# Two blocks' PV sums in one PSUM bank with one divide, and a later load of W2, in a two-layer sliding-window transformer kernel

## The chip, the cores and the metric

The kernel runs on one core of one Trainium2 chip. A core has TensorE (PE in profiles: matrix products out of SBUF into PSUM), VectorE (DVE), ScalarE (ACT), GpSimd (POOL) and SyncE (SP, which here issues all DMAs). The engines run side by side, each through its own instructions in order, and wait for each other on semaphores. The metric is the device time of one execution in microseconds (us), as the median of several runs.

## The reference

The same pair of layers is applied twice to x of 2048 rows by 512 columns: attention in a sliding window of 256 keys with 32 heads of 16, and a two-matrix block with a ReLU in between. Both follow a layer normalisation and are added to x.

```python
def _A_ref(x, wqkv, wo):                       # H = 32, Dh = 16, W = 256
    qkv = (x @ wqkv) -> q, k, v per head
    scores = einsum("bhqd,bhkd->bhqk", q, k) * (Dh ** -0.5)
    mask = (i - j >= 0) & (i - j < W)
    p = softmax(where(mask, scores, -1e9))
    return (p @ v, heads side by side) @ wo

def _B_ref(x, w1, w2):                         # Dff = 1792
    return relu(x @ w1) @ w2

x = x + _A_ref(layernorm(x), wqkv, wo)
x = x + _B_ref(layernorm(x), w1, w2)
x = x + _A_ref(layernorm(x), wqkv, wo)
x = x + _B_ref(layernorm(x), w1, w2)
```

Inputs and output are bfloat16; x is kept in float32 on the chip.

## The kernel before

**Tiles and stages.** The 2048 rows are cut into four chunks of 512. A step k = 0 to 7 is one chunk of one layer (k = 4 layer + chunk). Each step has three parts: `plan_qkv` (normalise, transpose, project to Q, K and V), `plan_attention`, and `plan_rest` (output projection wo, residual, normalise, transpose, W1 with ReLU, W2, residual). x, all weights, K and V stay in SBUF.

**Attention.** Heads are taken eight at a time (t = 0 to 3). A `Unit` is one t with all eight 64-row query blocks of a chunk, or, in the first and the last step, with four of them. Its scores come in up to five groups ("score blocks"), each of up to four times 512 columns in four PSUM banks (`Sps`). ScalarE takes the exponential of each block into one of two buffers `Pb`, which alternate from unit to unit. Triangular masks are laid over the edges by VectorE (a minimum with `tri`) or GpSimd (`affine_select`, two instructions for each edge). `pv_group` then multiplies with V: for each 128-row query block (`jl`, four in a full unit) and each of four head pairs p, up to six matmuls of 34 columns add into a tile `acc`. Columns 16 of each 17 hold the sums of the exponentials, since V carries a column of ones. `divide` (lines 393 to 398) takes the reciprocal of these sums into `chk` and multiplies 128 columns into `O`. Units are counted below from 0, in order of time.

**Transposes.** The normalised blocks `xn` (a pool of three buffers) are transposed by DMA into `xnT` and `xn2T`, the attention's output `O` into `OT`. Each is one `dma_start_transpose` on SP's queue, in the order in which SP stands. The first step's xn and the last step's O and xn go through TensorE instead (tiles `tp`).

**PSUM.** Four banks are for scores, four (pool `psum`, line 226) for everything else. A piece of work that needs one takes it at its first matmul and gives it back when the engine that empties it has finished. This holds for the accumulations over four or fourteen matmuls (`ps_d`), for the transposes and for `acc`.

**The order of the work.** A planner in the kernel makes it when the program is built. Each piece is an `Op` with a key, the engines that can do it with a cost in us, and what it depends on. The planner runs through time with these costs (lines 759 to 796): whenever an engine is free, it takes the ready piece with the lowest key. Score blocks and their exponentials have the lowest keys (-1e5), then PV sums (-5e4), final transposes, wo, then the projections and the W1 and W2 products, which fill what is left. Work that two engines can do (masks, copies out of PSUM, V copies, normalisations) goes to whichever comes first. When TensorE has had nothing for 0.4 us by the plan and more than one bank is free, a warming matmul on the identity (`warm`, 128 by 512) is put in until something is ready. On the chip, each engine then goes through its pieces in that order, whatever the real times. All instructions are made by one helper, so that profiles show them under line 106: tiles tell them apart.

**Loads.** SP issues them at the start in this order: x of chunk 0, the three parts of wqkv, x of the other chunks, wo, W1, W2 (lines 131 to 142). For the planner they land at fixed times (lines 237 to 240).

```python
d_wo, d_w1, d_w2 = landed(18.0), landed(24.0), landed(30.0)
...
box.ps = box.tile([P, 4, 2, 17], FP32, "acc")
```

In step 0, `plan_qkv(1)` comes right after the attention (line 676), so the normalised blocks of chunk 1 are the first that go through DMA transposes.

Of the kernel before, what the change touches and what calls it, by code (L numbers as in the profile page):

```python
# [9 lines left out]
FP32 = mybir.dt.float32  # L10
# [4 lines left out]
ALU = mybir.AluOpType  # L15
P = 128
# [46 lines left out]
def kernel(  # L63
# [51 lines left out]
    pe, dve, act, pool, sp = (InOrder(x) for x in (nc.tensor, nc.vector, nc.scalar, nc.gpsimd, nc.sync))  # L115

    def mm(o, lhsT, rhs, start, stop):
        pe.matmul(o, lhsT=lhsT, rhs=rhs, start=start, stop=stop)
# [20 lines left out]
    w1 = const.tile([P, KC, DFF], BF16, name="w1")  # L139
    sp.dma_start(w1[:], B_w1.rearrange("(kc p) n -> p kc n", p=P))  # L140
    w2 = const.tile([P, NF, D], BF16, name="w2")
    sp.dma_start(w2[:], B_w2.rearrange("(f p) n -> p f n", p=P))


    ident = const.tile([P, P], BF16, name="ident")
# [41 lines left out]
    SOON = {"qkv": 0, "v": 0, "h": 0, "mask": 0, "div": -1, "add": -1}  # L187
# [34 lines left out]
    def op(key, opts, deps=(), take=None, uses=(), keep=0):  # L222
        uses = list(uses) + ([take] if take is not None and take not in uses else [])
        return Op(key, opts, deps, take, uses, keep)
# [6 lines left out]
    def landed(t):  # L231
        o = Op(0, {}, [], None, [], 0)
        fixed.append((o, t))
        return o
# [2 lines left out]
    d_x = [landed(3.95), landed(4.5)]  # L237
    d_w = {1: landed(7.4), 0: landed(9.0), 2: landed(10.6)}
    d_xc = {c: landed(11.4 + 1.7 * c) for c in range(1, NCH)}
    d_wo, d_w1, d_w2 = landed(18.0), landed(24.0), landed(30.0)  # L240


    def copy(e, o, i, relu=False):
# [11 lines left out]
    def options(times, fn):  # L255
        return {e: (t, lambda e=e: fn(e)) for e, t in times.items()}
# [64 lines left out]
    def slot(layer, kb):  # L321
        return (32 * layer + kb) % NSLOT
# [20 lines left out]
    def score_group(u, g, Qt, pb, Sps):  # L343
        layer = u.k // NCH
        for kb, lo, n, at in u.groups[g]:
            sl = slot(layer, 8 * u.c + u.q0 + kb)
            for r in range(4):
                rows = slice(32 * r, 32 * r + 32)
                mm(Sps[:, r, 64 * at:64 * (at + n)], KBD[rows, u.t, sl].rearrange("p e k -> p (e k)"),
                   Qt[rows, 64 * (u.q0 + lo):64 * (u.q0 + lo + n)], True, True)  # L350

    def bounds(u, g):
        return 64 * min(b[3] for b in u.groups[g]), 64 * max(b[3] + b[2] for b in u.groups[g])

    def places(pb, g):
        return Pb[pb][:, 0:PWALL].rearrange("p (g r c) -> p g r c", g=5, r=4)[:, g]

    def exp_group(u, g, pb, Sps):
        a, z = bounds(u, g)
        act.activation(places(pb, g)[:, :, 64 + a:64 + z], Sps[:, :, a:z], ACT.Exp, scale=0.25)  # L360
# [21 lines left out]
    def seen(u, jl):  # L382
        return [kb for kb in range(2 * jl - 4, 2 * jl + 2) if u.c > 0 or kb + u.q0 >= 0]

    def pv_group(u, jl, p, pb, acc):
        kbs = seen(u, jl)
        for i, kb in enumerate(kbs):
            g, lo, at = u.place[kb]
            col = (4 * g + p) * PW + 64 + 64 * (at + 2 * jl - lo)
            mm(acc[:, p], Pb[pb][:, col:col + P], V2[:, slot(u.k // NCH, 8 * u.c + u.q0 + kb), :, 4 * u.t + p, :],  # L390
               i == 0, i == len(kbs) - 1)

    def divide(t, j, acc, O, chk):
        rinv = chk[:, j, 8 * t:8 * t + 8].rearrange("p (a e) -> p a e", e=2)
        dve.reciprocal(rinv, acc[:, :, :, 16])
        dve.tensor_tensor(out=O[:, j, P * t:P * (t + 1)].rearrange("p (a e d) -> p a e d", a=4, e=2),
                          in0=acc[:, :, :, 0:16],
                          in1=rinv.rearrange("p a (e o) -> p a e o", o=1).to_broadcast([P, 4, 2, 16]), op=ALU.mult)

    def accumulate_check(chk, first):  # L400
        mx = small.tile([P, 1], FP32, name="chk_mx")
# [27 lines left out]
    first_slot = {}  # L429
# [22 lines left out]
    scores, exps, masks, pvs, divs, checks = {}, {}, {}, {}, {}, []  # L452
    k_done, q_done, v_done, qkv_mm, w1_mm, w2_mm, x_done = {}, {}, {}, {}, {}, {}, {}
    applied, turned = {}, {}
    Q, xnTs, xn2T, hTs, O_of = {}, {}, {}, {}, {}

    def first(table, key, make):
        if key not in table:
            table[key] = make()
        return table[key]  # L460
# [71 lines left out]
    def plan_attention(k):  # L532
        layer, c = divmod(k, NCH)
        prev = units_of.get(k - 1, []) if c else []
        for n in units_of[k]:
            u = units[n]
            pb = n % 2
            before = [pvs[n - 2, j] for j in range(units[n - 2].nq // 2)] if n > 1 else [c_p[0], c_p[1]]
            for g in range(len(u.groups)):
                s = first_slot[n] + g  # L540
                h = u.q0 // 4 if k == 0 else 0
                need = [k_done[k, u.t, 0], q_done[k, u.t, h]] + ([k_done[k, u.t, 1]] if k == 0 and h else [])
                if c:
                    need += [k_done[k - 1, u.t, i] for i in range(2) if (k - 1, u.t, i) in k_done]
                cols = sum(b[2] for b in u.groups[g]) * 64
                a, z = bounds(u, g)
                cell = {}

                def sfn(u=u, g=g, pb=pb, cell=cell):
                    cell["S"] = ps_s.tile([P, 4, 512], FP32, name="Sps")  # L550
                    score_group(u, g, Q[u.k, u.t], pb, cell["S"])
                scores[s] = op(-1e5 + s, {"PE": (0.2 + 0.02 * len(u.groups[g]) + cols * 0.00042, sfn, 0.27 + 0.02 * len(u.groups[g]) + cols * 0.00042)},
                               need + ([exps[s - 1]] if s else []))
                exps[s] = op(-1e5, {"ACT": (0.168 + 0.00083 * 4 * (z - a), lambda u=u, g=g, pb=pb, cell=cell: exp_group(u, g, pb, cell["S"]))},
                             [scores[s]] + before)
                masks[s] = []
                for m in u.masks(g):
                    times = {"DVE": 0.32 + 0.14 * (len(m) - 1), "POOL": 0.93 * len(m)}
                    masks[s].append(op(SOON["mask"], options(times, lambda e, m=m, g=g, pb=pb: mask(e, m, places(pb, g))), [exps[s]] + c_tri))
            for jl in range(u.nq // 2):  # L560
                kbs = seen(u, jl)
                need = []
                for g in sorted({u.place[kb][0] for kb in kbs}):
                    need += [exps[first_slot[n] + g]] + masks[first_slot[n] + g]
                for kb in kbs:
                    b = u.q0 + kb
                    need.append(v_done[k, b // 2] if b >= 0 else v_done[k - 1, (b + 8) // 2])
                j = u.q0 // 2 + jl
                box = Box(psum)

                prior = None
                for p in range(4):
                    def pfn(u=u, jl=jl, pb=pb, box=box, p=p):
                        if p == 0:
                            box.ps = box.tile([P, 4, 2, 17], FP32, "acc")
                        pv_group(u, jl, p, pb, box.ps)
                    prior = op(-5e4 + n - (1000 if p else 0), {"PE": (0.025 * len(kbs) + (0.03 if p == 0 else 0.0), pfn)},
                               [prior] if p else need, None if p else box, [box])
                pvs[n, jl] = prior

                def dfn(u=u, j=j, box=box):
                    o = first(O_of, u.k, lambda: work.tile([P, 4, D], BF16, name="O", tag="O", bufs=1))
                    divide(u.t, j, box.ps, o, chks[u.k % 2])
                war = [turned[k - 1, i] for i in range(4)] if k else []
                divs[k, u.t, j] = op(SOON["div"], {"DVE": (0.5, dfn)}, [pvs[n, jl]] + war + checks[k - 2:k - 1], None, [box])
        checks.append(op(40, {"DVE": (1.1, lambda k=k: accumulate_check(chks[k % 2], k == 0))},
                         [divs[k, t, j] for t in range(4) for j in range(4)] + checks[-1:]))

# [84 lines left out]
    for k in range(NSTEP):  # L673
        plan_attention(k)
        if k == 0:
            plan_qkv(1)
        plan_rest(k)
        if 0 < k < NSTEP - 1:
            plan_qkv(k + 1)
# [80 lines left out]
    while events and events[0][0] < 3000:  # L760
        t, _, o, e = heapq.heappop(events)
# [15 lines left out]
        for e in ENGINES:  # L777
            if busy[e] > t + 1e-9:
                continue
            o = choose(e, t)  # L780
# [4 lines left out]
            elif e == "PE" and done_ops[0] < len(ops) - 12:  # L785
                if t - idle_since[0] >= (0.4 if t > 20 else 0.0) and sum(1 for f, _ in psum.free if f <= t) > 1:
                    box = Box(psum)
                    box.users = 1
                    d = Op(0, {"PE": (0.43 if t < 9 else 0.216, lambda: None)}, [], box, [], 0)
# [83 lines left out]
    with tc.If(flag > 0):  # L873
# [13 lines left out]
        for layer in range(2):  # L887
            for c in range(NCH):
# [13 lines left out]
                O = work.tile([P, 4, D], BF16, name="O", tag="O", bufs=1)  # L902
# [51 lines left out]
```

## Time and profile before

| what | us |
|---|---|
| median of 4 runs | 486.83 (486.37 to 487.46) |
| the profiled execution, whole | 486.64 |
| its span on the core | 484.9 |
| TensorE busy | 465.0 |
| VectorE busy | 368.4 |
| ScalarE busy | 337.7 |
| GpSimd busy | 316.8 |
| w loads, issue to landing (median of two) | 13.6 |
| DMA transposes, issue to landing (median) | 2.5 |

The span is the time from the first to the last instruction of the core; 1.7 us of the execution lie around it. Busy time of TensorE counts an instruction from its start to its modelled end, so that a busy TensorE need not be at its peak. In rows of the timeline, the first number is the start in us, the second how long the row lasts, xN how many instructions it merges, and the bracket how long the engine sat idle before it, with what ended the wait. In rows of the groups, the numbers behind the bar are busy us, mean ns of one, and idle us before.

### The profile page before, as it was taken

How to read it: one execution, taken by the hardware profiler on the slowest of the kernel's cores; microseconds unless marked ns; L12 is line 12 of the kernel's file. 1: busy time of each engine (PE TensorE's matmuls, PEld its weight loads, DVE VectorE, ACT ScalarE, POOL GpSimd, SP SyncE). 2: the span in 40 equal slices, each digit the busy share in tenths (PEclk: the TensorE clock that was granted, in tenths of full speed). 3: DMA queues.
4: the chain of work that ended last, by engine and by line, in shares of the span. 5: the costliest groups of instructions: out<-in, count | busy, mean ns of one | idle time of the engine just before them, and what ended most of it. 6: DMA issues, size and time to landing. Idle time of an engine off the chain costs nothing.

```text
span 484.9 us, 14677 instructions
## 1 busy us (share of the span) xinstructions
PE 465.0 (96%) x6055; PEld 249.8 (52%) x6055; DVE 368.4 (76%) x965; ACT 337.7 (70%) x281; POOL 316.8 (65%) x716
## 2 busy tenths in 40 slices
PE   8889899998999999999999999999999999999995
PEld 3554555654445545554544554455555455554662
DVE  6979989858897789878989977898768878463111
ACT  3857878878777767876778877777865676755341
POOL 7768878768886778777878767677656557631000
PEclk9989999999999999999999999999999999999999
DMA  8940131003300142002211023020143002100100
GB/s 276 369 56 17 36 55 24 3 1 57 71 8 3 23 67 45 3 1 45 58 34 31 15 34 47 12 46 1 27 85 57 13 1 46 34 12 13 34 23 28
DMA packets 54652, 22.00 MB, mean 45 GB/s; under 512 B 46129, under 2 KB 54065, under 8 KB 54577
## 3 DMA queue, kind: packets, MB, share of 16 engines
q1 hardware_dynamic: 54576, 20.98, 19.8%
q8 instruction: 49, 0.80, 0.7%
q14 instruction: 27, 0.21, 0.2%
HBM read 7.86 MB, written 2.10 MB: 21 GB/s over the span
## 4 chain that ended last, share of the span: by engine, by line
PE 75%; DVE 11%; DMA 8%; ACT 2%; POOL 2%; issue 1%; DVEq 0%; ACTq 0%; POOLq 0%
PE ps_d L106 54%; PE acc L106 12%; PE Sps L106 8%; DMA OT<-O 5%; DMA xnT<-xn 3%; ACT Pb L106 2%; DVE st L106 2%; DVE KBD L106 2%; DVE Pb L106 1%; DVE xn L106 1%; DVE x_sb L106 1%; POOL Pb L106 1%; DVE rstds L106 1%; POOL xn L106 1%; DVE V2f L106 1%
## 5 line engine op out<-in xcount | busy, mean ns | idle before, releaser
L106 ACT ACTIVATE Pb<-Sps 128x2048 bf16<-128x2048 f32 (+4 forms) x164 | 284.0, 1731 | 96.4 <-PE Sps L106 72.5
L106 POOL TENSOR_SCALAR_AFFINE_SELECT Pb<-Pb 64x256 bf16<-64x256 bf16 x526 | 227.2, 432 | 95.8 <-ACT Pb L106 73.1
L106 PE MATMUL ps_d<-xn2T,w 128*128 128x512 bf16 (+1 forms) x560 | 110.4, 337 | 0.9 <-DVE hT L106 0.9
L106 PE MATMUL ps_d<-w,hT 128*128 128x512 bf16 x448 | 110.0, 380 | 0.0
L106 PEld LDWEIGHTS <-Pb 128*128 128x128 bf16 x2880 | 83.3, 96 | 24.7 <-issue 7.5
L106 PE MATMUL acc<-V2f,Pb 128*128 128x34 bf16 x2880 | 89.9, 178 | 2.2 <-POOL Pb L106 1.1
L106 PEld LDWEIGHTS <-w 128*128 128x128 bf16 x560 | 50.8, 97 | 39.1 <-issue 4.4
L106 PE MATMUL ps_d<-xnT,wqkv 128*128 128x512 bf16 (+1 forms) x288 | 67.7, 362 | 3.2 <-DVE O L106 1.4
L106 PE MATMUL Sps<-Qt,KBD 32*128 32x192 bf16 (+4 forms) x1536 | 62.5, 249 | 2.6 <-ACT Pb L106 2.4
L106 DVE TENSOR_TENSOR Pb<-Pb,tri 128x512 bf16<-128x512 bf16 (+1 forms) x136 | 58.2, 432 | 7.4 <-ACT Pb L106 7.1
L106 PEld LDWEIGHTS <-hT 128*128 128x128 bf16 x448 | 39.9, 97 | 44.2 <-issue 2.8
L106 DVE TENSOR_SCALAR hT<-ps_d 128x512 bf16<-128x512 f32 (+1 forms) x76 | 47.0, 626 | 11.1 <-PE ps_d L106 10.5
L106 PEld LDWEIGHTS <-KBD 32*128 32x128 bf16 x1536 | 25.7, 92 | 53.5 <-issue 50.5
L106 DVE TENSOR_SCALAR KBD<-ps_d,par 128x256 bf16<-128x256 f32 (+1 forms) x82 | 45.5, 605 | 1.1 <-PE ps_d L106 0.9
L106 ACT ACTIVATE hT<-ps_d 128x256 bf16<-128x256 f32 (+1 forms) x64 | 29.6, 466 | 22.7 <-PE ps_d L106 21.1
L106 DVE BATCH_NORM_STATS2 st<-x_sb 128x6 f32<-128x512 f32 (+1 forms) x64 | 43.8, 684 | 1.0 <-DMA x_sb<-in_A_x_dram 0.5
L106 DVE TENSOR_TENSOR x_sb<-ps_d,x_sb 128x512 f32<-128x512 f32 x48 | 32.8, 685 | 14.3 <-PE ps_d L106 13.8
L106 DVE TENSOR_TENSOR O<-acc,chk 128x128 bf16<-128x128 f32 x128 | 37.3, 291 | 4.5
L106 PEld LDWEIGHTS <-wqkv 128*128 128x128 bf16 x288 | 26.4, 99 | 27.8 <-issue 5.2
L106 DVE RECIPROCAL chk<-acc 128x8 f32<-128x8 f32 x128 | 25.6, 200 | 18.3 <-PE acc L106 15.8
L106 PE MATMUL ps_d<-wo,OT 128*128 128x512 bf16 x128 | 32.9, 380 | 4.0 <-DMA OT<-O 3.7
L106 DVE TENSOR_TENSOR ob<-ps_d,x_sb 128x512 bf16<-128x512 f32 x16 | 11.0, 688 | 31.5 <-PE ps_d L106 31.5
(55 smaller groups left out, 301.8 us busy)
## 6 DMA issues: line engine op xcount, KB each, us to landing
w<-in_B_w_dram SPq DMA_DIRECT2D x2, 1792.0 KB, 13.6
out_dram<-ob SPq DMA_DIRECT2D x16, 128.0 KB, 1.7
wqkv<-in_A_wqkv_dram SPq DMA_DIRECT2D x3, 512.0 KB, 6.4
x_sb<-in_A_x_dram SPq DMA_DIRECT2D x3, 512.0 KB, 9.3
x_sb<-in_A_x_dram SPq DMA_DIRECT2D x2, 256.0 KB, 2.9
wo<-in_A_wo_dram SPq DMA_DIRECT2D x1, 512.0 KB, 8.9
xnT<-xn SPq DMA_TRANSPOSE x28, 2.5
OT<-O SPq DMA_TRANSPOSE x28, 2.5
```

The lines of the kernel that those rows point to most:

```text
L106: inst = fn(*a, **k)
```

## The change

**The divide.** Two neighbouring 128-row query blocks (`j0` and `j0 + 1`) share one tile `acc`, which is now 128 x 2 x 4 x 2 x 17 values (1088 bytes a partition). The bank is taken at the first sums of the first block, the second block's sums follow in the same bank, and one reciprocal of 16 values and one product of 256 empty it. The planner's cost for it is 0.64 in place of 0.5, and one `Op` stands for the divides of both blocks. The number of PV matmuls is the same.

**W2.** Its load leaves the head of SP's queue and becomes a piece of work on SP that depends on the four transposes of chunk 1 (`applied[2]`), with 1.4 us for the issue and 9.0 until it has landed as the planner's costs.

```diff
-    sp.dma_start(w2[:], B_w2.rearrange("(f p) n -> p f n", p=P))
...
-    d_wo, d_w1, d_w2 = landed(18.0), landed(24.0), landed(30.0)
+    d_wo, d_w1 = landed(18.0), landed(24.0)
...
     def divide(t, j, acc, O, chk):
-        rinv = chk[:, j, 8 * t:8 * t + 8].rearrange("p (a e) -> p a e", e=2)
-        dve.reciprocal(rinv, acc[:, :, :, 16])
-        dve.tensor_tensor(out=O[:, j, P * t:P * (t + 1)].rearrange("p (a e d) -> p a e d", a=4, e=2),
-                          in0=acc[:, :, :, 0:16],
-                          in1=rinv.rearrange("p a (e o) -> p a e o", o=1).to_broadcast([P, 4, 2, 16]), op=ALU.mult)
+        sums = acc[:].rearrange("p j a e d -> p j (a e) d")
+        rinv = chk[:, j:j + 2, 8 * t:8 * t + 8]
+        dve.reciprocal(rinv, sums[:, :, :, 16])
+        dve.tensor_tensor(out=O[:, j:j + 2, P * t:P * (t + 1)].rearrange("p j (a d) -> p j a d", d=16),
+                          in0=sums[:, :, :, 0:16],
+                          in1=rinv.rearrange("p j (a o) -> p j a o", o=1).to_broadcast([P, 2, 8, 16]), op=ALU.mult)
...
-            for jl in range(u.nq // 2):
+            for j0 in range(0, u.nq // 2, 2):
+                box = Box(psum)
                 prior = None
+                for jl in (j0, j0 + 1):
+                    kbs = seen(u, jl)
+                    need = [prior]
+                    ...
+                    for p in range(4):
+                        begins = jl == j0 and p == 0
+                        def pfn(u=u, jl=jl, j0=j0, pb=pb, box=box, p=p, begins=begins):
+                            if begins:
+                                box.ps = box.tile([P, 2, 4, 2, 17], FP32, "acc")
+                            pv_group(u, jl, p, pb, box.ps[:, jl - j0])
+                        prior = op(-5e4 + n - (0 if begins else 1000),
+                                   {"PE": (0.025 * len(kbs) + (0.03 if p == 0 else 0.0), pfn)},
+                                   need if p == 0 else [prior], box if begins else None, [box])
+                    pvs[n, jl] = prior
+                j = u.q0 // 2 + j0
...
-                divs[k, u.t, j] = op(SOON["div"], {"DVE": (0.5, dfn)}, [pvs[n, jl]] + war + checks[k - 2:k - 1], None, [box])
+                divs[k, u.t, j] = divs[k, u.t, j + 1] = op(
+                    SOON["div"], {"DVE": (0.64, dfn)}, [prior] + war + checks[k - 2:k - 1], None, [box])
...
         if k == 0:
             plan_qkv(1)
+            d_w2 = op(0, {"SP": (1.4, lambda: sp.dma_start(w2[:], B_w2.rearrange("(f p) n -> p f n", p=P)), 9.0)}, applied[2])
```

The planner makes its order anew with these pieces, so the instructions of every engine stand in another order than before throughout. In the built program GpSimd has 492 mask instructions (526 before) and 56 V copies (64), VectorE 72 V copies (64), and TensorE 44 warming matmuls (38). On SP the fourth transpose of chunk 1 is followed by the load of W2, and this by the first two OT transposes.

## The prediction

> **What bounds the kernel now.** First the page's busy rows and the granted clock by slices.
>
> ```profile
> PE 465.0 (96%) x6055; PEld 249.8 (52%) x6055; DVE 368.4 (76%) x965; ACT 337.7 (70%) x281; POOL 316.8 (65%) x716
> PEclk9989999999999999999999999999999999999999
> ```
>
> TensorE is busy for 465.0 of 484.9 us. Of its 19.9 us of idle time, 4.9 us lie behind the last matmul and 1.5 us ahead of the first, so about 13 us can be won in between, and the 16 warming matmuls in the middle of the run (0.216 us each, from the 512-column rows that follow each other) hide another 3.5 us. One slice has a lower clock. Next, the timeline from 20 to 32 us, and the windows of one microsecond there (columns: window, PE, PEld, DVE, ACT, POOL busy, clock, DMA share, GB/s).
>
> ```profile
> 21.40 7.48 SPq L106 DMA_TRANSPOSE xnT<-xn  x4
> 22.22 2.82 POOL L106 TENSOR_SCALAR_AFFINE_SELECT Pb<-Pb 64x256 bf16<-64x256 bf16 x6
> 25.06 0.61 PE L106 MATMUL ps_d<-xnT,wqkv 128*128 128x256 bf16 x4
> 25.10 1.72 POOL L106 COPY V2f<-Vst 64x256 bf16<-64x256 bf16 x4
> 26.88 4.68 POOL L106 TENSOR_SCALAR_AFFINE_SELECT Pb<-Pb 64x256 bf16<-64x256 bf16 x10
> 26.99 0.45 DVE L106 TENSOR_SCALAR xn<-x_sb,mvs,rstds 128x512 bf16<-128x512 bf16 x1 [1.87 <-DMA xnT<-xn]
> 27.93 2.72 PE L106 MATMUL ps_d<-xnT,wqkv 128*128 128x256 bf16 x12 [1.43 <-DVE O L106]
> 30.58 0.61 PE L106 MATMUL Sps<-Qt,KBD 32*128 32x192 bf16 x12
> 33.03 0.36 PE L106 MATMUL acc<-V2f,Pb 128*128 128x34 bf16 x8
> 33.89 0.41 PE L106 MATMUL Sps<-Qt,KBD 32*128 32x64 bf16 x16 [0.28 <-ACT Pb L106]
> ```
>
> ```profile
> 27.00:28.00 1.00, 0.07 (x1) 0.07 (x1) 0.97 (x4) 1.00 (x1) 0.89 (x3) 0.82 0.22 35
> 28.00:29.00 1.00, 1.00 (x6) 0.67 (x6) 0.97 (x4) 0.28 (x2) 0.87 (x3) 0.50 0.34 66
> ```
>
> This is one story. There are three xn buffers. The fourth normalised block of chunk 1 waits on VectorE for the first transposing DMA, which was issued at 21.40 and landed at 26.97: 5.57 us, where the median of these transposes is 2.5 us. VectorE is in order, so the divide behind it came late, a PSUM bank stayed taken, and TensorE waited 1.43 us. Then its clock fell to half: twelve 256-column matmuls took 2.72 us, 0.227 each, where the four at 25.06 stand (0.61 - 0.27)/3 = 0.113 apart (0.27 is the duration of one).
>
> Last, the chunk boundary at 116 to 126 us, where most of the other middle idle time lies, and the rows that the divide edit touches.
>
> ```profile
> 116.56 1.24 PE L106 MATMUL warm<-ident 128*128 128x512 bf16 x5
> 119.33 1.90 PE L106 MATMUL ps_d<-wo,OT 128*128 128x512 bf16 x8 [0.93 <-DMA OT<-O]
> 125.43 1.67 PE L106 MATMUL ps_d<-xnT,wqkv 128*128 128x512 bf16 x7 [0.89 <-DMA xnT<-xn]
> ```
>
> ```profile
> L106 DVE TENSOR_TENSOR O<-acc,chk 128x128 bf16<-128x128 f32 x128 | 37.3, 291 | 4.5
> L106 DVE RECIPROCAL chk<-acc 128x8 f32<-128x8 f32 x128 | 25.6, 200 | 18.3 <-PE acc L106 15.8
> L106 DVE TENSOR_TENSOR x_sb<-ps_d,x_sb 128x512 f32<-128x512 f32 x48 | 32.8, 685 | 14.3 <-PE ps_d L106 13.8
> ```
>
> From 130 to 430 us TensorE idles for only 4.2 us in all (0.74, 0.78, 0.25, 0.67, 0.21, 0.86 and 0.67), and behind the last score block some 52 us of matmuls (at the rows' rates) are left in either program. The change can win only in the first 130 us and in those 4 us.
>
> **The change part by part.**
>
> **1. W2 behind chunk 1's transposes.** The load is one issue on SP (1.65 us, mean of the two w rows) and 1792 KB, in about 5.0 us at the 350 to 380 GB/s of the windows around 20 us. Ahead of the transposes it is in the same queue; behind them, the first finds only w1 in front, which by the same rate lands near 21 us. I take 2.5 us for it: landing at 23.9. In the built program the fourth normalisation is then no longer on VectorE but on GpSimd, behind the six mask instructions that end at 25.04; with its two small products it takes some 1.6 us (as at 20.43 to 22.25), to 26.7, and waits for no buffer. So VectorE's 1.87 us wait goes, and with it TensorE's 1.43 us of idle time and 12 x (0.227 - 0.113) = 1.37 us of half clock; with 0.2 us for the slower score block, 3.0 us. That is the upper end. The lower is what GpSimd makes late next. Its masks now follow the normalisation and the V copies (1.72 us, to 28.4): two instructions for unit 2 and four for unit 3, at 0.45 us, end near 31.1, where in the old order the ten ended at 31.56. The PV sums of unit 3 can then run whole at 31.2 to 31.85 instead of 33.03 to 34.65; three projection matmuls (0.65) follow, and the next score block stands at 32.5 instead of 33.89, with 16 PV matmuls more behind it (0.026 us each, 0.41). Gain 1.4 + 0.4 = **1.8 us**; ends 0 (GpSimd later than so) and 3.0.
>
> What hides W2 itself: its first matmul is at 65.3 us. Issued after the fourth transpose, at about 28, it lands near 35: 30 us to spare. What stands behind it on SP is the first OT transpose (issued at 34.8 before, used at 38.5). The Trainium skill, "DMA: Bandwidth & Descriptors" (Queues, rings and completion order), says that each DMA engine consumes a queue's descriptors in ring order; this speaks against the change, since OT now stands behind 1.8 MB. The row agrees for xnT (5.57 for 2.5). By the rule alone OT would be up to 3 us late if it were issued straight behind W2, and the 1.8 us would be gone; by the times of the rows, six microseconds lie between W2's issue and OT's, and it costs nothing to 1 us. I take 0.
>
> Of the clock, the skill's "TensorE: Matmul & The Clock Gate" (What's actually happening) says that a cold state comes after an idle window of about 3.4 us. The row shows half clock after gaps of 0.41, 0.45 and 1.43 us within 4 us. By the page these 1.37 us aren't tied to the stall, and part 1 would be worth at most 1.65; by the row they are. The row decides.
>
> **2. Paired divide.** 128 x (0.200 + 0.291) = 62.8 us become 64 reciprocals of 16 and 64 products of 256 elements. The slope between the products of 128 and 512 elements out of PSUM is (685 - 291)/384 = 1.03 ns; so 0.422 and 0.208 us, 40.3 us in all, 22.5 us off VectorE. It is not the bound, and part of the room fills: the built program takes 34 mask instructions (0.43 us each) and 8 V copies (0.42) off GpSimd. Where VectorE is nearly full (9.77 of 10 us at 40 to 50), four pairs save 4 x 0.35 = 1.4 us, against TensorE waits of 0.28, 0.24 and 0.89 there: I take **0.3**. Of the waits after 130 us, four name VectorE or GpSimd (0.74, 0.67, 0.21, 0.86: 2.5 us); a third is **0.8 us**; ends 0 and 2.5.
>
> **3. What pairing delays.** A pair's bank is taken at the first block's sums and freed after the second's. By the program's order and the rows' rates TensorE does on average 2.13 us of work between a bank's first and last PV matmul, where it was 0.66, of four banks. Also block 0 of a chunk is divided with block 1, one score block (some 2.4 us) later, and so is its OT transpose. At the boundary of chunks 1 and 2 the built program shows it: the four wo matmuls that ran at 115.27 to 116.5 stand one block later, and the warming matmuls between 90 and 105 us of matmul work are 14 instead of 8. That is 6 x 0.216 = 1.3 us, and the three more holes that they start in could add as much. Against it stand the waits of 0.93 and 0.89 us that the trace has there and that a later wo takes up, and the score block at 118.00, which waits for its exponentials (0.20 us, by the timeline) whatever TensorE does: **+0.6**, ends 0 and 2.5. At the other boundaries the last OT is 0.14 us later by the longer divide, and up to four transposes at 1.2 to 1.5 us go out in one row; other matmuls stand in front of wo there: **+0.3**, ends 0 and 1.5.
>
> Sum: -1.8 - 0.3 - 0.8 + 0.6 + 0.3 = -2.0 us. The profiled execution took 486.64 us (span 484.9 and 1.7 around it), 0.19 us below the median of 486.83; its difference carries over: **484.8 us**.
>
> **The rivals.** About 0.2% (1.0 us) is what a measurement of this kernel can tell from no change.
>
> *Gain given back.* GpSimd takes the stall over (part 1 worth 0 to 1), and the longer hole at chunk 2 costs 1.3: 486.5. For it: GpSimd is at 0.87 to 0.96 through this stretch and gets the normalisation on top. Against: it loses four mask instructions of unit 2 to VectorE just there.
>
> *Slower: bank held too long.* With one of four banks held three times as long, evacuations have three, and a divide that VectorE does late stops TensorE, as at 27.93. Over the 56 pairs behind the head, 2.0/56 = 0.036 us a pair eat the gain, from 0.054 on the kernel is over 1 us slower, and 0.08, which I take, gives 484.8 + 4.5 = 489.3. For it: that one wait exists. Against: it is the only one of its kind in the trace, and came from the DMA.
>
> *VectorE's relief is worth more.* All 2.5 us of waits go (1.7 more than taken), and 3.0 in the head (1.2 more): 481.9.
>
> **How the numbers follow.** The forecast 0.52, given back 0.16, slower 0.22, more 0.10. The likeliest's own range, with its ends partly added, is 483 to 486. The range for 8 in 10 leaves out the outer half of the slower case and little of the better one: 482.2 to 488.0. Faster: 0.10, 0.46 of the forecast and 0.02, 0.58; the same: 0.06 + 0.13 + 0.01 = 0.20; slower 0.22.
>
> **What would show it.** The first xnT transpose lands 2.5 us after its issue and no xn waits on DMA there; the clock slice at 24 to 36 us has no dip; the first block of sixteen 64-column score matmuls comes near 32.5 us. The products show near 0.42 us. At 115 to 126 us more warming matmuls, wo later. Wrong would be: waits of ps_d for the divide (bank) through the dense part, or the clock falling again at 26 to 31 us.

## The result and the profile after

| | before | changed |
|---|---|---|
| median, us | 486.96 (55 runs) | 485.71 (35 runs, 483.52 to 487.86) |
| ratio to before, 95% interval | 1 | 0.9973 [0.9964, 0.9982] |
| span of the profiled execution, us | 484.9 | 484.1 |
| end of the last matmul in it, us | 479.9 | 478.3 |

The change makes the kernel 1.3 us faster (0.9 to 1.8). The forecast was 2.0 us. The profile's first part and the row of the granted clock (in tenths, by fortieths of the span; before, it had an 8 in the third place):

```profile
PE 463.5 (96%) x6061; PEld 249.2 (51%) x6061; DVE 358.2 (74%) x850; ACT 338.9 (70%) x283; POOL 302.3 (62%) x677
PEclk9999999999999999999999999999999999999999
```

The dip of the clock is gone in this execution. VectorE has 10.2 us less to do, GpSimd 14.5 us. The timeline of the changed kernel where the wait and the half clock were (the columns are those of the timelines above):

```profile
21.38 6.12 SPq L106 DMA_TRANSPOSE xnT<-xn  x4
27.56 1.95 SPq L106 DMA_DIRECT2D w<-in_B_w_dram  x1
28.60 0.40 PE L106 MATMUL Sps<-Qt,KBD 32*128 32x192 bf16 x12 [0.83 <-ACT Pb L106]
30.71 1.02 PE L106 MATMUL ps_d<-xnT,wqkv 128*128 128x512 bf16 x4 [1.01 <-DVE O L106]
32.93 0.40 PE L106 MATMUL Sps<-Qt,KBD 32*128 32x64 bf16 x16
33.84 2.50 SPq L106 DMA_TRANSPOSE OT<-O  x2
38.36 1.04 PE L106 MATMUL ps_d<-wo,OT 128*128 128x512 bf16 x4 [0.81 <-DMA OT<-O]
```

The block of sixteen 64-column score matmuls comes at 32.93 (32.5 forecast, 33.89 before). But the wait for a divide is not gone: 1.43 us became 1.01 us, and 0.83 us of waiting for an exponential came in front of it. And the first OT transpose, issued at 33.84, was used at 38.36: 4.5 us, where the median of the OT transposes is 2.5. W2, issued at 27.56, stood ahead of it and took 10.3 us to land. In the five traces where OT is issued 4 to 7 us behind W2 and lands late (the changed kernel and experiments 1, 5, 6 and 8), it took between 4.1 and 5.8 us and landed 0.5 us behind W2 in each; in experiments 4 and 12, where W2 itself landed sooner (in 8.7 and 8.1 us), OT took 3.0 and 2.4. The boundary of chunks 1 and 2, and the worst wait further on:

```profile
114.88 1.90 PE L106 MATMUL warm<-ident 128*128 128x512 bf16 x8
118.59 2.33 PE L106 MATMUL ps_d<-wo,OT 128*128 128x512 bf16 x10 [1.22 <-DMA OT<-O]
121.63 0.81 PE L106 MATMUL warm<-ident 128*128 128x512 bf16 x3
...
176.56 0.82 PE L106 MATMUL ps_d<-wo,OT 128*128 128x512 bf16 x3 [1.59 <-DMA OT<-O]
```

The divide's two instructions, as groups of the tile `acc` (durations in ns: least, median, greatest):

```profile
L106 DVE RECIPROCAL chk<-acc x64: 225/257/259, 22.2 to 430.2; 128x16 f32<-128x16 f32 x64
L106 DVE TENSOR_TENSOR O<-acc,chk x64: 423/424/426, 22.5 to 430.4; 128x256 bf16<-128x256 f32 x64
```

The product takes the 0.42 us forecast, the reciprocal 0.257 instead of 0.208: 64 x 0.681 = 43.6 us instead of 40.3, so that the divides take 19.2 us less of VectorE than before (62.8) and not 22.5.

A measure used below is the lead: how much earlier than before the exponential of a score block starts, "block 8" being the ninth of the 164. At the last one only the closing matmuls are left in every kernel, so the lead there compares whole kernels; in between, kernels have done more or less of the other work, and a lead shows only where time is lost.

### The profile page after: what moved, and what is told of

Read it like the earlier page. It is cut to its first block, busy times and chain, and to the rows that moved or that the text cites. A ratio compares the mean times of both kernels' runs of the same rounds, so it can differ in the third digit from the quotient of the medians.

```text
span 484.1 us, 14517 instructions
## 1 busy us (share of the span) xinstructions
PE 463.5 (96%) x6061; PEld 249.2 (51%) x6061; DVE 358.2 (74%) x850; ACT 338.9 (70%) x283; POOL 302.3 (62%) x677
## 4 chain that ended last, share of the span: by engine, by line
PE 78%; DVE 10%; DMA 5%; POOL 2%; ACT 2%; issue 1%; POOLq 0%; ACTq 0%; DVEq 0%
PE ps_d L106 55%; PE acc L106 14%; PE Sps L106 9%; DMA OT<-O 4%; DVE KBD L106 2%; DVE st L106 2%; ACT Pb L106 2%; DVE V2f L106 1%; DVE Vst L106 1%; DVE Pb L106 1%; DVE x_sb L106 1%; POOL xn L106 1%; POOL Pb L106 1%; DVE O L106 1%; DMA x_sb<-in_A_x_dram 1%
## 5 line engine op out<-in xcount | busy, mean ns | idle before, releaser
L106 POOL TENSOR_SCALAR_AFFINE_SELECT Pb<-Pb 64x256 bf16<-64x256 bf16 x492 | 214.3, 436 | 106.2 <-ACT Pb L106 83.1
L106 DVE TENSOR_TENSOR Pb<-Pb,tri 128x512 bf16<-128x512 bf16 (+1 forms) x144 | 62.5, 440 | 13.4 <-ACT Pb L106 12.3
L106 DVE TENSOR_SCALAR hT<-ps_d 128x512 bf16<-128x512 f32 (+1 forms) x72 | 44.6, 625 | 13.7 <-PE ps_d L106 13.3
L106 ACT ACTIVATE hT<-ps_d 128x256 bf16<-128x256 f32 (+1 forms) x68 | 32.0, 473 | 24.4 <-PE ps_d L106 22.6
L106 DVE TENSOR_SCALAR KBD<-ps_d,par 128x256 bf16<-128x256 f32 (+1 forms) x80 | 44.1, 602 | 2.3 <-PE ps_d L106 2.2
L106 PE MATMUL ps_d<-wqkv,xnT 128*128 128x512 bf16 x128 | 34.0, 380 | 0.7 <-DVE O L106 0.4
L106 POOL TENSOR_TENSOR rstds<-rstds,mhalf 128x2 f32<-128x2 f32 (+1 forms) x33 | 23.6, 718 | 16.8 <-DVE rstds L106 15.0
```

The lines of the kernel that those rows point to most:

```text
L106: inst = fn(*a, **k)
```

## The experiments

Four questions. What is each part worth alone? Was the wait on VectorE the cause of the half clock? What do the pairs cost, a late OT or a bank held long? And does the new order by itself matter, since the planner makes all of it anew when one cost changes?

**1. W2's load alone.** Only the load is moved; all other instructions stand where they stood before.

```
-    sp.dma_start(w2[:], ...)                  # at the start
+            d_w2 = op(0, {"SP": (1.4, lambda: sp.dma_start(w2[:], ...), 9.0)}, applied[2])
```

> The kernel before with only the load of W2 moved behind the four transposes of chunk 1; every other instruction stands where it stood. Theory A (the stall at 25 to 31 us comes from W2 standing ahead of the transposes, and is on the path that sets the end): the first xnT transpose lands about 2.5 us after its issue, no xn waits on a DMA there, the clock stays whole, and the time falls by 1.5 to 3.0 us. Rival B (GpSimd's ten masks, which end at 31.56 either way, hold the PV sums, so that the stall costs nothing): the waits move, the time stays within 0.5 us of before. Rival C (the gain of the change is the divide's): also within 0.5 us.

Measured: 484.22 us, ratio 0.9954 [0.9939, 0.9970], 2.2 us faster. The six runs' median lies 3.2 us below that of all the executions of before listed with it (487.40); here as below, gains are taken from the ratios on record. The lead is 2.41 us at block 8 and 3.43 at the last block (1.66 in the changed kernel). The wait for the divide is down to 0.24 us, and the block of sixteen score matmuls comes at 32.13:

```profile
29.73 1.46 PE L106 MATMUL ps_d<-xnT,wqkv 128*128 128x512 bf16 x6 [0.24 <-DVE O L106]
```

The first OT transpose is late here too (issued at 32.67, landed at 36.85), but TensorE had other matmuls until 36.90. Part 1 alone gives more than the whole change, and the rivals B and C are out.

**2. The pairs alone.** The changed kernel with W2's load back at the start.

```
+    sp.dma_start(w2[:], ...)                  # at the start, as before
-            d_w2 = op(0, {"SP": (1.4, lambda: sp.dma_start(w2[:], ...), 9.0)}, applied[2])
```

> The changed kernel with W2 back at the head of the queue; every other instruction stands as in the changed kernel, pairing and its divide stay. Theory A (pairing is worth about nothing, -0.2 us in the forecast's sum, since the relief of VectorE and the later OT cancel): within 1 us of before. Rival C (the gain of the change is the divide's): about 1.3 us faster than before. Rival D (pairing by itself costs, and the later W2 pays for it): 0.5 to 2 us slower than before.

Measured: 487.68 us, ratio 1.0011 [0.9998, 1.0024], 0.5 us slower if anything. That leaves theories A and D, and not C. The lead of 0.63 us at the last block of its profile says the same within the spread of the runs. So the two parts are -2.2 and +0.5; their sum, -1.7, and the -1.3 of the whole agree within the intervals.

**3. The fourth normalised block in a spare buffer.** W2 stays at the start and the transposes stay late; only VectorE's wait for a free xn buffer is taken away, with an OT buffer that is idle then.

```
-            box.t = box.tile([P, D], BF16, "xn")
+            box.t = (work.tile([P, D], BF16, name="xn", tag="OT2", bufs=1)
+                     if lid == 2 and j == 3 else box.tile([P, D], BF16, "xn"))
```

> The kernel before with W2 at the head, but the fourth normalised block of chunk 1 goes into a buffer that is idle then (the third OT buffer), so that VectorE has nothing to wait for; the transposes still stand behind W2. It tells apart whether VectorE's wait or the late transposes cost. If the wait (theory A): TensorE's 1.43 us wait and the half clock go, 1.5 to 3 us faster than before. If the late xnT (the projections of chunk 1 start late whatever VectorE does): TensorE waits for DMA xnT in its place, within 0.5 us of before.

Measured: 485.45 us, ratio 0.9970 [0.9955, 0.9985], 1.5 us faster. So most of the 2.2 us of the first experiment comes from VectorE's wait and what hangs on it; some 0.7 us would be left for the late transposes themselves, but that difference lies within the two intervals. The clock did not fall in its profile, although TensorE still waited 1.20 us for a divide:

```profile
30.78 1.46 PE L106 MATMUL ps_d<-xnT,wqkv 128*128 128x512 bf16 x6 [1.20 <-DVE O L106]
```

**4. Four instructions for each pair.** The changed kernel's order and banks, but each pair is divided by two reciprocals of 8 and two products of 128.

```
+        for h in range(2):
+            rinv = chk[:, j + h, 8 * t:8 * t + 8].rearrange("p (a e) -> p a e", e=2)
+            dve.reciprocal(rinv, acc[:, h, :, :, 16])
+            dve.tensor_tensor(out=O[:, j + h, ...], in0=acc[:, h, :, :, 0:16], in1=..., op=ALU.mult)
```

> The changed kernel in its own order, but each paired divide is done by two reciprocals of 8 and two products of 128 in place of one of 16 and one of 256: about 19 us more work on VectorE and nothing else. Theory A (the relief of VectorE was counted at 1.1 us): 0.5 to 1.5 us slower than the changed kernel, so near before. If VectorE is nowhere on the path: as the changed kernel, within 0.3 us. If its relief is the main thing: 2 us or more slower than the changed kernel, so slower than before.

Measured: 486.86 us, ratio 1.0001 [0.9988, 1.0014]. Against the changed kernel's 0.9973 that is 1.3 us (some 0.6 to 2.1, by the two intervals): what the shorter VectorE time is worth in this order. The divides take 62.9 us here, 43.4 in the changed kernel. In its profile the clock fell at 31.0 us; the section on the clock takes that up. From 130 to 435 us, where the clock did not fall, TensorE's waits that name VectorE make 1.5 us, where the changed kernel, in the same order, has 0.4 (columns: total us, times, longest):

```profile
PE ps_d L106 <- DVE hT L106: 0.7, 1, 0.7
PE acc L106 <- DVE Pb L106: 0.3, 1, 0.3
PE ps_d L106 <- DVE KBD L106: 0.3, 1, 0.3
PE ps_d L106 <- DVE O L106: 0.2, 1, 0.2
```

**5. Pairs only of blocks that need the same scores.** Blocks 2 and 3 of a full unit, and both blocks of a half unit: 40 pairs and 48 single blocks. Blocks 0 and 1 are divided as early as before.

```
-            for j0 in range(0, u.nq // 2, 2):
+            for j0, step in ((0, 1), (1, 1), (2, 2)) if u.nq == 8 else ((0, 2),):
```

> W2 late as in the change; of each chunk's sixteen query blocks only those are paired whose sums need no further score block (blocks 2 and 3 of a unit of four, and the two of a half unit): 40 pairs and 48 single blocks instead of 64 pairs. A bank is held for 1.0 us of TensorE work between its first and last sums (0.66 before, 2.13 in the changed kernel), and the first two query blocks of a chunk are divided as early as before. Theory A, the pairing loses by what it delays (the early block waits for the later one's scores, its bank and its OT with it): the loss goes and some relief of VectorE stays, 482.8 to 484.2 us, not slower than the kernel with W2 alone moved (0.9954 of before). Theory B, the hold costs little and a new order of the instructions moves the time by a microsecond either way: anywhere from 483.5 to 486.5. Theory C, the two longer instructions themselves cost: about 485.0, between W2 alone and the changed kernel.

Measured: 484.59 us, ratio 0.9942 [0.9930, 0.9954]. The loss of the full pairing is gone, as theory A had it; but the point also lies in theory B's range (a new order), and experiment 8 gives that theory weight, so this run does not show the cause. The kernel with W2 alone (0.9954) is not told apart from it.

**6. Pairs in three of the four groups of heads.** The last group, which completes O and lets OT go, has single blocks.

```
+            step = 1 if u.t == 3 else 2
-            for j0 in range(0, u.nq // 2, 2):
+            for j0 in range(0, u.nq // 2, step):
```

> W2 late; pairs in the first three of the four groups of heads, single blocks in the last. OT's divides of the last group come as early as before, the banks are still held long (1.61 us of TensorE work on average, where it was 0.66 before and 2.13 in the changed kernel). Theory A1, the late OT at the boundary of chunks 1 and 2 is what pairing costs: the 2.0 us lost there come back, about 484.0. Theory A2, the held banks are what costs: only (2.13-1.61)/(2.13-0.66) = a third of 1.8 us comes back, about 485.2. Theory B, it is the order made anew: no relation to either.

Measured: 486.63 us, ratio 0.9985 [0.9966, 1.0004]. Neither A1 nor A2 had it. Its timeline on SP and TensorE shows what happened (durations of 512-column matmuls show the clock):

```profile
32.04 2.65 SPq L106 DMA_TRANSPOSE OT<-O  x2
...
34.82 0.29 PE L106 MATMUL Sps<-Qt,KBD 32*128 32x256 bf16 x4
37.86 1.04 PE L106 MATMUL ps_d<-wo,OT 128*128 128x512 bf16 x4 [2.75 <-DMA OT<-O]
38.73 0.71 PE L106 MATMUL ps_d<-wqkv,xnT 128*128 128x512 bf16 x2
39.38 0.61 PE L106 MATMUL Sps<-Qt,KBD 32*128 32x192 bf16 x12
39.92 1.89 PE L106 MATMUL ps_d<-wo,OT 128*128 128x512 bf16 x4
```

O is ready earlier, so the wo matmuls stand earlier in TensorE's order, at 35.1. But OT, issued at 32.04, is there only at 37.86, 5.8 us later, with W2's 1.8 MB in front of it. TensorE waits 2.75 us, and from 39.1 the clock is at half: four matmuls of 512 columns take 1.89 us, where the four at 37.86 took 1.04. This asked for experiments 9 and 10.

**7. W2 behind the first OT transposes.** The changed kernel's own order; W2's load is issued right after OT's second transpose. Experiments 9 and 10 have the same edit.

```
-            d_w2 = op(0, {"SP": (1.4, lambda: sp.dma_start(w2[:], ...), 9.0)}, applied[2])
+            d_w2 = op(0, {"SP": (1.4, lambda: None, 9.0)}, applied[2])
...
+                    if k == 0 and j == 1:      # after OT's transpose of block 1
+                        sp.dma_start(w2[:], ...)
```

> The changed kernel in its own order, with the load of W2 issued behind the first two OT transposes instead of ahead of them; nothing else moves. Theory A, OT stood behind W2's 1.8 MB in the queue and TensorE waited 0.81 us for it at 38.4: OT lands about 2.5 us after its issue instead of 4.5, the wait is gone, 0.5 to 0.9 us faster than the changed kernel (ratio to before 0.9955 to 0.9965). Theory B, the wait only moves to what comes behind it in the dense stretch: the same as the changed kernel, 0.997.

Measured: 486.42 us, ratio 0.9981 [0.9964, 0.9999]. The wait for OT is gone from the trace, as theory A said, yet no time is won. Two things stand against it. TensorE's waits at 53 us for a mask on GpSimd grew from 0.60 to 1.19 us, as theory B said. And the clock fell at 30.9 us, ahead of the edit, where the order is the changed kernel's:

```profile
28.61 0.40 PE L106 MATMUL Sps<-Qt,KBD 32*128 32x192 bf16 x12 [0.83 <-ACT Pb L106]
28.94 0.77 PE L106 MATMUL acc<-V2f,Pb 128*128 128x34 bf16 x24
30.80 0.56 PE L106 MATMUL ps_d<-xnT,wqkv 128*128 128x512 bf16 x1 [1.09 <-DVE O L106]
31.58 1.06 PE L106 MATMUL ps_d<-xnT,wqkv 128*128 128x512 bf16 x2 [0.22 <-issue]
```

(From experiment 5 on, about 75 matmul records of 6060 are missing in each trace; the 0.22 us is one of them.) The changed kernel reached the sixteen-matmul block at 32.93, this one at 34.44. The same program stretch, with gaps that differ by 0.08 us, kept its clock in one execution and lost it in the other.

**8. The same work in a new order.** W2 late and single blocks, as in the first experiment, but the planner reckons a divide at 0.64 us, the cost that the change gave it.

```
-                divs[k, u.t, j] = op(SOON["div"], {"DVE": (0.5, dfn)}, ...)
+                divs[k, u.t, j] = op(SOON["div"], {"DVE": (0.64, dfn)}, ...)
```

> The kernel with W2 alone moved (0.9954 of before), with its divides still of one block each, but planned at 0.64 instead of 0.50 us each, so that the same work comes in a different order. Theory B, a new order by itself moves the time by a microsecond either way: 483 to 487, outside 0.9940 to 0.9968 of before. Theory A, the order made by the planner matters little, and what the pairing lost it lost by its banks and by its later OT: within 0.9940 to 0.9968 of before.

Measured: 488.09 us, ratio 1.0012 [0.9997, 1.0027]: 2.8 us slower than the same work in the order before. Theory A is out; theory B had the cause, but with a microsecond either way too small a size. Its profile has two stretches of half clock, at 31.4 and 55.3 us, which cost 3.4 us together (half of TensorE's busy time in them). But the order costs without them too: the five executions whose mean granted clock is 0.997 or more have a median of 486.65 us, against 484.22 for W2 alone, whose six all have such a clock. In the profile TensorE waits 6.8 us for exponentials and 4.7 us for OT (2.5 and 2.2 with W2 alone). So what this kernel wins or loses by one replanned cost is as large as what the change was forecast to bring.

**9. Same-score pairs, W2 behind OT.** Experiment 5 with the edit of experiment 7.

> The kernel that pairs only blocks with the same scores (0.9942 of before), in its own order, with W2's load issued behind the first two OT transposes instead of ahead of them. Theory A, OT stands behind W2 in the queue: the wait of 0.54 us for OT at 37.4 us goes and nothing takes its place, 0.9932 of before (484.1 us). Theory B, the wait only moves: 0.9942 as before.

Measured: 483.63 us, ratio 0.9929 [0.9908, 0.9950]. The wait of 0.54 us is gone from the trace and the point lies where theory A had it; the intervals of 5 and 9 overlap.

**10. Pairs in three groups, W2 behind OT.** Experiment 6 with the edit of experiment 7.

> The kernel with pairs in the first three groups of heads (0.9985 of before), in its own order, with W2's load issued behind the first two OT transposes. In its trace TensorE waited 2.75 us for OT at 35.1 us, and the clock then fell to half for 3.4 us (1.7 us lost). Theory A, both come from OT standing behind W2: 2.5 to 4.4 us faster, 482.2 to 484.1 us, 0.9895 to 0.9935 of before, and its long-held banks cost nothing that shows. Theory B, the order itself is bad and the banks are held too long: less than 1.5 us come back, 0.9955 or more.

Measured: 482.96 us, ratio 0.9907 [0.9891, 0.9922]: 4.5 us faster than before, 3.8 us faster than experiment 6, and the lowest median here (its interval overlaps that of experiment 9). The same stretch of its timeline:

```profile
32.32 2.50 SPq L106 DMA_TRANSPOSE OT<-O  x2
34.87 0.57 SPq L106 DMA_DIRECT2D w<-in_B_w_dram  x1
...
35.09 0.29 PE L106 MATMUL Sps<-Qt,KBD 32*128 32x256 bf16 x4
35.32 1.04 PE L106 MATMUL ps_d<-wo,OT 128*128 128x512 bf16 x4
```

The wo matmuls follow without a wait. That is the clearest single result, in one and the same order of the engines: one DMA issue moved past two others was worth 3.8 us here, and nothing measurable in experiment 7. (The clock is in it: its mean over the executions is 0.9919 in experiment 6 and 0.9948 here, which is 1.4 us in 485 at most.) The lead at the last block is 5.23 us (3.43 with W2 alone), so pairs can gain. But the boundary of chunks 1 and 2 is no better than in the changed kernel: 1.90 us of waiting for OT at 119.07. A1's place for the gain was wrong.

**11. A gap filled.** Experiment 7's kernel, with four matmuls done twice just ahead of the 0.83 us gap.

```
                     mm(ps[:, cols], wqkv[...], xnT[0][:, kc, cols], kc == 0, kc == KC - 1)
+                    if k == 0 and h == 1 and t == 3 and kc == KC - 1:
+                        for i in range(KC):      # the same four again, into the same bank
+                            mm(ps[:, cols], wqkv[...], xnT[0][:, i, cols], i == 0, i == KC - 1)
```

> The changed kernel with W2 behind the first two OT transposes (0.9981 of before; in its trace the clock fell to half at 30.9 us, after gaps of 0.83 and 1.09 us), and four matmuls of 256 columns done twice in one group, just ahead of the gap of 0.83 us, which they fill to a half; nothing else moves. Theory A, the sum of the gaps decides whether the clock falls: it stays full although there is more work, 1.2 to 1.5 us faster than without, 0.9950 to 0.9957 of before. Theory B, the clock's fall has nothing to do with the gaps, or the later evacuation makes the second gap longer: 0.9981 or above.

Measured: 486.09 us, ratio 0.9970 [0.9958, 0.9982]. Its trace, one execution, is as theory A had it: the gap is 0.39 us, nothing behind it is later, and the clock stays full.

```profile
28.61 0.40 PE L106 MATMUL Sps<-Qt,KBD 32*128 32x192 bf16 x12 [0.39 <-ACT Pb L106]
28.94 0.77 PE L106 MATMUL acc<-V2f,Pb 128*128 128x34 bf16 x24
30.70 1.02 PE L106 MATMUL ps_d<-xnT,wqkv 128*128 128x512 bf16 x3 [0.99 <-DVE O L106]
```

The time is 0.5 us better than in experiment 7, less than expected, and the intervals overlap, so the time alone does not show it. The section on the clock gives a reason why it should be less.

**12. Chunk 0 as before, same-score pairs from chunk 1 on.** W2 late.

```
-            for j0 in range(0, u.nq // 2, 2):
+            for j0, step in [(i, 1) for i in range(u.nq // 2)] if k == 0 else (
+                    ((0, 1), (1, 1), (2, 2)) if u.nq == 8 else ((0, 2),)):
```

> W2 late; chunk 0 with single blocks, in the same order as the kernel with W2 alone moved; from chunk 1 on only blocks with the same scores are paired. Theory A, pairs that delay nothing gain by VectorE's relief where TensorE waits for it: the start of the kernel with W2 alone (2.3 us ahead of before by the 24th exponential) and the rest of the kernel that pairs same-score blocks (another 1.6 us from there on): 483.5 us, 0.992 of before. Theory B, VectorE's relief is worth nothing where no bank is short: 0.9954 as with W2 alone.

Measured: 483.76 us, ratio 0.9921 [0.9903, 0.9939]. The point is theory A's; its interval and that of W2 alone [0.9939, 0.9970] just touch. Its profiled execution was one of 487.28 us, with a mean granted clock of 0.992, while the other six runs took 482.66 to 484.60 with 0.997 to 0.999; the trace has two stretches of half clock, 3.3 us together. Without them it would be at 484.0, with the rest: so the fall of the clock is a part of the spread from run to run.

## Why the prediction was right, and where not

The direction and the range held. The sum had -2.0, the runs have -1.3 [-1.8, -0.9]. That the sum came this near is in part luck: the first of its terms was 0.4 us too small and the cost of pairing 0.9 us too small, and the two errors work against each other. By its steps:

**W2 behind the transposes: -1.8 forecast, -2.2 [-3.0, -1.5] alone.** Right, and for the reason given (experiment 3: the wait on VectorE is most of it), with a part in the clock that the next section sizes. In the changed kernel the lead at block 8 is 2.19 us.

**W2 ahead of OT: 0 taken, 0 to 1 as its span.** The rule of the Trainium skill that was weighed there, "DMA: Bandwidth & Descriptors" (Queues, rings and completion order), was right against this kernel: OT waited for 1.8 MB issued 6.3 us before it. The step that was off is "six microseconds lie between W2's issue and OT's, and it costs nothing to 1 us". The forecast had W2, issued at about 28, land near 35; issued at 27.56, it landed at 37.8. Its transfer did not start with its issue: the DMA queue moved 8 GB/s from 29 to 30 us and 286 to 353 GB/s from 31 to 36, and the fourth xnT transpose, ahead of it, landed at 30.6. So there are 10.8 us from W2's issue to OT's landing. The price was 0.81 us in the changed kernel and, with the wo matmuls a little earlier, 2.75 us and a fall of the clock (experiments 6 and 10: 3.8 us). In the changed kernel itself 0.81 us lies within the 0 to 1 that the forecast allowed, and taking it away (experiment 7) brought nothing at the end: in that trace the wait for the mask at 53 us grew by 0.6 us.

**VectorE's relief: -1.1 forecast, -1.3 measured** (experiment 4, within some 0.6 to 2.1), though the reciprocal was reckoned 0.05 us too cheap. The waits that TensorE has between 130 and 432 us, from the changed kernel and from W2 alone (columns: total us, times, longest):

```profile
PE ps_d L106 <- DMA OT<-O: 2.1, 2, 1.6
PE ps_d L106 <- DMA xn2T<-xn: 0.4, 1, 0.4
PE ps_d L106 <- DVE O L106: 0.4, 1, 0.4
```

```profile
PE ps_d L106 <- DMA OT<-O: 1.3, 4, 0.4
PE acc L106 <- DVE Pb L106: 0.9, 1, 0.9
PE ps_d L106 <- DVE hT L106: 0.7, 1, 0.7
PE acc L106 <- POOL Pb L106: 0.5, 1, 0.5
```

The waits that name VectorE or GpSimd fell from 2.1 to 0.4 us: not a third of them, as taken, but nearly all. With the longer divides in the changed kernel's order they are back at 1.5 (experiment 4), so most of the fall is the relief and not the order. Waits for OT came instead.

**What pairing delays: +0.6 and +0.3 forecast, +1.8 by the runs** (experiment 2's +0.5 less the -1.3 of the relief, each known to some 0.7 us; what the new order costs by itself is in it). This is the term that was mis-sized. The six more warming matmuls came as forecast (44 instead of 38, 1.3 us). Of the two waits set against them, which a later wo was to take up, only one went: that for xnT at 125 us (0.89 us). The one for OT grew from 0.93 to 1.22 us. Corrected for the other work done by then, at the rows' rates, the lead falls by 2.0 us from block 40 to block 44, of which about 1.0 is back by block 60; with W2 alone it stays. At 176 us the wait for OT is 1.59 (0.78 at 170 us before). The waits of all wo matmuls for OT, in the changed kernel and with W2 alone:

```profile
L106 PE MATMUL ps_d<-wo,OT 128*128 128x512 bf16 x128 | 33.6, 380 | 4.3 <-DMA OT<-O 4.2
```

```profile
L106 PE MATMUL ps_d<-wo,OT 128*128 128x512 bf16 x128 | 32.9, 380 | 2.7 <-DMA OT<-O 2.2
```

Between the two traces, 2.0 us more of waiting for OT, 1.3 us more of warming and, behind 130 us, 1.7 us less of waiting for VectorE and GpSimd make 1.6; the last matmul ends 1.8 us later (478.3 and 476.5). The account is not complete: ahead of 130 us, the wait for a divide is 0.8 us longer and that for xnT 0.9 us shorter, and smaller ones differ too.

**The rivals.** "Bank held too long" priced 4.5 us over the dense part; the wait for a divide is 0.4 us in all there, and experiment 10, with banks held for 1.61 us on average, has the lowest median. It shows at one place, at 30.7, where the projection waits 1.01 us for a pair's divide and 0.24 with W2 alone. "Gain given back" described the chunk boundary rightly. GpSimd did not take the stall over: the waits of 0.83 and 1.01 us name ScalarE's exponential and VectorE's divide.

**What stays open.** How much of the changed kernel's loss is the late OT and how much the planner's order can't be said: each kernel that pairs differently also has a new order, and experiment 8 shows 2.8 us from order alone. It is not the clock: the 27 executions of the changed kernel with a mean granted clock of 0.997 or more have a median of 485.66 us, still 1.4 us above W2 alone.

## What the runs showed of the clock

The ten stretches of half clock ahead of the last matmul in these traces (before and the experiments) show more than the gaps that the prediction went by. Each lasts 3.4 us. In one execution they lie on a fixed grid: from 31.44 to 55.34 in experiment 8 are 7.00 times 3.4133 us, from 39.08 to 124.42 in experiment 6 25.00 times, from 118.96 to 170.16 in experiment 12 15.00 times, and from 30.86 in experiment 7 to the fall after its last matmul at 481.42 132.00 times. This is the free-running window of the Trainium skill's "TensorE: Matmul & The Clock Gate" (What's actually happening), and these traces agree with its length of 3413 ns. They do not agree that the window has to be idle, as the page's table has it. Windows on the grid of each execution (columns: window, its length, PE, PEld, DVE, ACT and POOL busy, the granted clock, DMA share, GB/s), first experiment 7:

```profile
27.45:30.86 3.41, 1.49 (x40) 1.09 (x39) 3.18 (x9) 2.46 (x3) 3.04 (x8) 1.00 0.54 43
30.86:34.27 3.41, 3.19 (x30) 1.47 (x31) 1.57 (x3) 0.80 (x1) 1.77 (x5) 0.50 0.00 0
34.27:37.69 3.42, 3.37 (x32) 1.46 (x33) 2.76 (x6) 2.19 (x2) 0.75 (x2) 1.00 0.34 65
```

and the changed kernel:

```profile
25.44:28.85 3.41, 2.10 (x38) 1.42 (x34) 3.38 (x10) 3.02 (x4) 3.11 (x7) 1.00 0.79 76
28.85:32.26 3.41, 2.40 (x64) 1.77 (x54) 2.22 (x6) 1.88 (x1) 2.31 (x7) 1.00 0.58 172
32.26:35.68 3.42, 3.42 (x37) 1.37 (x32) 3.22 (x8) 1.88 (x1) 1.46 (x4) 1.00 1.02 321
```

In experiment 7 both gaps lie in one window, TensorE is busy for 1.49 of 3.41 us, and the next window runs at half. In the changed kernel the edge of a window, at 28.85, lies between the gaps, and neither window is below 2.10. Over all traces, before and changed included, from 20 us to the window in which the last matmul ends, all eight windows with less than 1.83 us of busy TensorE were followed by half clock; with 1.86 or more, two were (1.97 and 2.18), and several with about 2.0 were not. (Where a matmul record is missing, a value can be 0.2 us low. Of the last windows themselves, one with 1.71 was not followed by half clock.) So busy time alone does not give a sharp bound. A fall costs 1.5 to 1.7 us, half of TensorE's busy time in it.

As the grid has another offset in each execution, a stall of this size should cost a chance and not a sum. An estimate: laid over each trace at 24 offsets, with a bound of 1.85 us, a window between 20 and 45 us falls below it at 13 offsets before, at 7 in the changed kernel, at 9 in experiment 7, and at none in experiments 1 and 11. By this, experiment 11 should gain 9/24 of 1.55 us, 0.6, on experiment 7, and it gained 0.5.

The mean granted clock, listed for each execution, tests the estimate. A whole window at half clock takes 0.0035 off it (half of 3.41 in 485 us); a fall behind the last matmul, which costs no time, takes up to about 0.004 in these traces. So 0.997 or more means no fall ahead of the end, and 0.995 or less means one at least.

| | executions | 0.997 or more | 0.995 or less | mean |
|---|---|---|---|---|
| before (beside the experiments) | 116 | 1 | 94 | 0.9938 |
| changed (the 35 of the median and two more) | 37 | 27 | 5 | 0.9975 |
| W2 alone (1) | 6 | 6 | 0 | 0.9982 |
| spare buffer (3) | 22 | 16 | 5 | 0.9974 |
| four-step divide (4) | 14 | 9 | 2 | 0.9973 |
| W2 behind OT (7) | 14 | 7 | 4 | 0.9961 |
| gap filled (11) | 12 | 8 | 2 | 0.9970 |

The estimate is of the right size for the changed kernel, W2 alone and experiment 7. It is too low for experiment 11, and far too low for before, whose clock fell in nearly every execution and not in half of them. So the stalls of one trace and one bound do not give the chance. What makes before fall so often is VectorE's wait for the buffer: experiment 3 takes away only that, and 5 of its 22 executions certainly fell. The forecast put the clock's 1.37 us wholly into its upper end; it was a price that before paid almost always. From before to the changed kernel the mean clock rises by 0.0037, which is 1.8 us in 485 at most, more than the whole gain of 1.3 us; with W2 alone it is 0.0044 or 2.1 us, beside a gain of 2.2. The gain can thus be largely the half clock that came with the stall; no run parts this from the wait itself. The longer divides of experiment 4 have the changed kernel's mean clock, so its 1.3 us is not the clock's.

## What to carry to other kernels

When a load is moved back in a queue, look at what then stands behind it and count from the first byte's turn to the last one's landing, not from the issue; and when a load is moved at all, put it behind the last thing that is needed soon: what it costs depends on how early the engine asks (3.8 us in experiment 10, nothing that shows in 7). Where a planner or a scheduler makes the order, an edit to a cost is an edit to everything: keep one variant in which nothing else moves, or its gain can't be told from the order's. A stall that empties about half of one 3.4 us window can cost as much again in clock, so read the stalls of a profile in pairs that could share a window, and ask the clock of all executions, not of one trace, how often the price is paid.
